# A new order for the lead-in of a gated linear attention with a folded maxout layer

## The chip, the cores and the metric

The kernel runs on one core of one Trainium2 chip. The metric is the device time of one execution in microseconds (us). Three runs of the kernel before gave 145.63, 147.28 and 148.08 us; their median is 147.28 us. One more execution was recorded by the hardware profiler; all durations below come from it.

## What is computed

For each of 4 batches and 8 heads (head size 48, 768 steps) a state of 48 x 48 is decayed by a gate and fed with an outer product, and then read:

```python
f = 1.0 / (1.0 + np.exp(-f_logit))
state = f[:, :, t, :, None] * state + np.einsum('bhd,bhe->bhde', k[:, :, t], v[:, :, t])
y[:, :, t] = np.einsum('bhd,bhde->bhe', q[:, :, t], state)
```

The 3072 x 384 result x then goes through a maxout layer of width 1024:

```python
h1 = x @ w1
h2 = x @ w2
g = np.maximum(h1, h2)
return (g @ w_out).astype(np.float32)
```

Inputs and output are float32.

## The kernel before, in words

**Tiles.** The 768 steps of a batch are cut into 6 chunks of 128. A tile i is chunk i // 4 of batch i % 4, so there are 24 tiles; tiles 0 to 3 have no earlier state. Within a tile the recurrence is written as products of matrices: the logarithms of the gates are summed along the chunk by a product with a triangular matrix (p_cum, L215), k and q are scaled by the exponentials of that sum (ei and ed; m_kp L248, m_qp L253), both are transposed by TensorE (p_tr, L258), their product a (p_a, L274) is masked (v_am, L284), and y (p_y, L313) is the masked product with v, with the old state added from the second chunk on. The state of the next chunk comes from sa (p_sa), tmp (v_tmp) and st (m_st, on GpSimd).

**The maxout layer.** max(h1, h2) is h2 + relu(h1 - h2). With wd = w1 - w2 (sub_wd, L178) a tile needs d = wd' x' in two halves of 512 rows (p_d, L343), a relu on ScalarE (a_g, L353), and then o = x · (w2 · w_out) + g · w_out (p_o, L359). The product w2 · w_out, called w2o, is made once at the start: w2 is cast to bf16 (cast_w2, L168), transposed in 8 blocks (tr_w2 L183, ev_w2T L188), w_out is cast in 4 parts (cast_wo, L174), and 12 pairs of products are summed (mm_w2o L191, ev_w2o L199).

**What sets the order.** The work of every engine is an order written out by hand as text. A word names an operation and a number its tile or part: "d0 -1" in the steady step is the first half of d for the tile before. PROLOGUE (L17) covers the start, STEP (L41) is repeated for i from FIRST_STEP on, and EPILOGUE (L48) ends it. The dictionary ops (in the function's last part) maps words to functions, and run (L435) leaves out what was already done. Each engine works through its own instructions in that order and waits at each for its inputs; nothing overtakes on VectorE, ScalarE or GpSimd. Transfers are issued from SP's queue: f, k, q and v of a tile (load, L147), a weight block of 128 rows (load_w, L156), half of w_out (load_wo, L159). A load is 192 KB in rows of 192 bytes, with nine buffers for each of the four inputs. In the steady step the store of tile i - 4 is issued from ScalarE ("outa"), all loads from SP: v two tiles ahead, q and k three, f four. The gate's last row of a tile from FL_ROW on is moved by a small transfer (a_fl, L232: "fl").

**The lead-in.** VectorE sets up masks and zeroed buffers; the f, q, k, v of tile 0 and the blocks of w2 are loaded first, then w_out in two halves, then w1. Nine products of zeros ("warm", L403) keep TensorE working. The suffixes name engines: w2ca is the cast on ScalarE, wdp the subtraction on GpSimd, kpv and qpv the scalings on VectorE (kp and qp without it: GpSimd).

PSUM has three pools: three buffers "s" for the attention, one "a", and three "mm" for the maxout layer and for w2's transposes.

Of the kernel before, what the change touches and what calls it, by code (L numbers as in the profile page):

```python
# [484 lines left out]
```

## Time and profile before

| What | Value |
|---|---|
| Median of three runs | 147.28 us (145.63 to 148.08) |
| Profiled execution | 145.47 us, of it the span 143.4 us |
| TensorE matmul busy | 129.9 us (91%) |
| VectorE busy | 107.0 us (75%) |
| ScalarE busy | 87.2 us (61%) |
| GpSimd busy | 69.0 us (48%) |
| Moved by transfers | 28.62 MB, mean 200 GB/s |
| A steady tile on TensorE | 4.90 us |

The span is the time between the first and the last instruction that the profile shows; the execution's own time is 2.07 us longer. A busy TensorE counts a product at half clock as busy, so its share is read together with the granted clock. In the listings, "L357" is the line of the kernel, "gT<-d" says which tile is written from which, "x48" how many instructions, and "idle before" with an arrow names what ended the wait. Transfers have no engine of their own in the listing; their issues stand under SPq and ACTq.

### The profile page before, as it was taken

The numbers are of one execution on the slowest core, as the hardware profiler recorded it, in microseconds if no ns is written. First come the engines' busy times: TensorE is split into PE (matmuls) and PEld (weight loads), VectorE is DVE, ScalarE is ACT, GpSimd is POOL, SyncE is SP. The second block draws the span as 40 slices with busy tenths as digits, with TensorE's granted clock in tenths as the row PEclk, the third lists the DMA queues.
The fourth block names the chain that finished last, engine by engine and source line by source line (L and its number), as shares of the span: only waits on it lengthen the run. The fifth ranks groups of instructions, "written<-read, shape, count | busy, mean of one in ns | idle before, by whom it ended". The sixth has DMA issues, their size and how long they took to land.

```text
span 143.4 us, 4345 instructions
## 1 busy us (share of the span) xinstructions
PE 129.9 (91%) x1756; PEld 100.3 (70%) x1756; DVE 107.0 (75%) x191; ACT 87.2 (61%) x183; POOL 69.0 (48%) x98
## 2 busy tenths in 40 slices
PE   0197499999999999999999999999999999999981
PEld 0044357688778877877887788778878887887771
DVE  7835985796889788877977897798779777976520
ACT  3572545967577566748666765767585757663440
POOL 8520060220748386566657655855685546442000
PEclk9999959999999999999999999999999999999999
DMA  4999999999999997998999999999999999971111
GB/s 94 274 347 389 342 307 169 188 198 166 188 175 179 194 209 202 218 196 190 221 191 207 197 204 218 224 172 235 228 210 189 218 214 220 171 215 59 55 55 55
DMA packets 105763, 28.62 MB, mean 200 GB/s; under 512 B 101520, under 2 KB 104720, under 8 KB 105744
## 3 DMA queue, kind: packets, MB, share of 16 engines
q1 hardware_dynamic: 103728, 25.60, 87.4%
q10 hardware_dynamic: 2016, 2.75, 5.7%
q8 instruction: 13, 0.21, 0.6%
q14 instruction: 6, 0.05, 0.1%
HBM read 23.59 MB, written 4.72 MB: 197 GB/s over the span
## 4 chain that ended last, share of the span: by engine, by line
PE 80%; DMA 10%; SPq 5%; ACT 3%; issue 1%; DVE 1%
PE o L368 27%; PE d L350 23%; PE tr L263 7%; DMA wo_f<-in_moe_w_out_dram 6%; PE a L281 5%; DMA ft<-in_f_logit_dram 4%; PE w2op L196 4%; PE y L326 3%; PE xtp L336 3%; PE cum L218 3%; PE y L321 2%; PE sa L295 2%; SPq L152 2%; SPq L161 1%; SPq L157 1%; ACT wo L176 1%
## 5 line engine op out<-in xcount | busy, mean ns | idle before, releaser
L350 PE MATMUL d<-xT,wd 128*128 128x128 bf16 x576 | 43.4, 220 | 0.5 <-DVE xT L340 0.4
L256 POOL TENSOR_TENSOR qp<-qt,ed 128x384 bf16<-128x384 f32 x22 | 22.1, 1002 | 45.0 <-ACT ed L230 30.3
L350 PEld LDWEIGHTS <-wd 128*128 128x128 bf16 x576 | 36.5, 114 | 4.5 <-issue 0.9
L368 PE MATMUL o<-wo,gT 128*128 128x384 bf16 x184 | 37.4, 325 | 0.0
L357 ACT ACTIVATE gT<-d 128x512 bf16<-128x512 f32 x48 | 28.9, 603 | 9.6 <-PE d L350 9.4
L286 DVE TENSOR_TENSOR am<-a,mask 128x1024 bf16<-128x1024 f32 x24 | 29.4, 1224 | 1.4 <-PE a L281 0.9
L340 DVE COPY xT<-xtp 128x384 bf16<-128x384 bf16 x24 | 8.6, 358 | 18.9 <-PE xtp L336 18.9
L368 PEld LDWEIGHTS <-gT 128*128 128x128 bf16 x184 | 16.2, 97 | 9.0
L310 POOL TENSOR_TENSOR st<-tmp,fl 64x192 bf16<-64x192 f32 x40 | 21.2, 530 | 2.7
L230 ACT ACTIVATE ed<-cum 128x384 f32<-128x384 f32 x24 | 11.8, 493 | 16.1 <-PE cum L218 15.0
L272 DVE COPY trs<-tr 128x1024 bf16<-128x1024 bf16 (+1 forms) x27 | 17.0, 631 | 4.1 <-PE tr L263 2.3
L331 ACT CAST x<-y 128x384 bf16<-128x384 f32 x24 | 11.5, 478 | 12.2 <-PE y L326 12.2
L237 POOL COPY flrow<-ed 32x384 f32<-32x384 f32 x16 | 17.8, 1113 | 1.0
L368 PE MATMUL o<-w2o,xT 128*128 128x384 bf16 x69 | 15.0, 326 | 0.0
L205 ACT ACTIVATE e<-ft 128x384 f32<-128x384 f32 x24 | 12.5, 525 | 3.6 <-DMA ft<-in_f_logit_dram 3.6
L251 DVE TENSOR_TENSOR kp<-kt,ei 128x384 bf16<-128x384 f32 x23 | 14.1, 614 | 0.7 <-ACT ei L226 0.5
L218 PE MATMUL cum<-ell,ut 128*128 128x384 bf16 x24 | 8.1, 339 | 7.0 <-ACT ell L209 7.0
L209 ACT ACTIVATE ell<-e 128x384 bf16<-128x384 f32 x24 | 12.5, 524 | 0.7
L373 DVE COPY ob<-o 128x384 f32<-128x384 f32 x23 | 12.6, 547 | 0.0
L226 ACT ACTIVATE ei<-cum 128x384 f32<-128x384 f32 x24 | 11.9, 496 | 0.0
L326 PE MATMUL y<-vb,am 128*128 128x48 bf16 x192 | 11.3, 184 | 0.2 <-DVE vb L213 0.2
L326 PEld LDWEIGHTS <-am 128*128 128x128 bf16 x192 | 9.7, 96 | 2.3 <-DVE am L286 0.4
(58 smaller groups left out, 173.1 us busy)
## 6 DMA issues: line engine op xcount, KB each, us to landing
ft<-in_f_logit_dram SPq DMA_DIRECT2D x24, 192.0 KB, 4.7
qt<-in_q_dram SPq DMA_DIRECT2D x24, 192.0 KB, 4.4
kt<-in_k_dram SPq DMA_DIRECT2D x24, 192.0 KB, 4.4
vt<-in_v_dram SPq DMA_DIRECT2D x24, 192.0 KB, 4.6
w_f<-in_moe_w_dram SPq DMA_DIRECT2D x6, 512.0 KB, 6.9
out_dram<-ob ACTq DMA_DIRECT2D x14, 192.0 KB, 3.4
out_dram<-ob SPq DMA_DIRECT2D x9, 192.0 KB, 2.6
wo_f<-in_moe_w_out_dram SPq DMA_DIRECT2D x2, 768.0 KB, 8.2
```

The costliest lines, as they stand in the source:

```text
L205: nc.scalar.activation(e, ld[i]["f"].rearrange("p h d -> p (h d)"), AF.Exp, scale=-1.0)
L237: nc.gpsimd.tensor_copy(row[:, :, 0:D, :].rearrange("s o d p -> s p o d"), st[i]["ed"][96:C, :].rearrange("s (p o d) -> s p o d", p=NP, o=2))
L251: eng.tensor_mul(s["kp"][:, :, 0:D], ld[i]["k"], s["ei"].rearrange("p (h d) -> p h d", h=H))
L256: eng.tensor_mul(s["qp"][:, :, 0:D], ld[i]["q"], s["ed"].rearrange("p (h d) -> p h d", h=H))
L272: nc.vector.tensor_copy(s["tr"][:, n:n + len(sel)], psum.pop(("tr" + sel, i)))
L286: nc.vector.tensor_mul(am.rearrange("p o n c -> p (o n) c"), psum.pop(("a", i)).rearrange("p o n c -> p (o n) c"), mask)
L310: nc.gpsimd.tensor_mul(st_b[b][(c + 1) % 2][r, :, e], st[i]["tmp"][r, :, e], st[i]["fl"][r, :].unsqueeze(2).to_broadcast([DP, NP, D]))
L326: nc.tensor.matmul(out=y[:, ds], lhsT=am[:, o, p, :], rhs=vb[:, ds], start=(c == 0), stop=(c == 0 or o == 1))
L350: nc.tensor.matmul(out=psum["d", half, i][:, n, :], lhsT=wd[:, j, ff(half * 4 + n)], rhs=st[i]["xT"][:, j, :], start=(j == 0), stop=(j == ...
L357: nc.scalar.activation(s["g"][:, half * 4:half * 4 + 4, :], psum.pop(("d", half, i)), AF.Relu)
L368: nc.tensor.matmul(out=psum["o", i], lhsT=l() if callable(l) else l, rhs=r, start=(n == 0), stop=(n == len(mms) - 1))
L373: nc.vector.tensor_copy(t, psum.pop(("o", i)))
```

## The change

The lead-in (the first four tiles and the weights) has another order, and the steady step starts at tile 4 instead of 7. w1 is loaded in halves of its columns and subtracted in halves (wdh on VectorE, wdhp on GpSimd). All w2 casts are on VectorE; the w_out casts are spread over VectorE (wocv), GpSimd (wocp) and ScalarE (woc); copies of w2's transposes and of w2o may be on ScalarE or VectorE (w2Tea, w2oev); v of tiles 1 to 3 is cast on ScalarE (va). Some transposes of w2 use the attention's PSUM buffers (w2Ts). q, k and v of some early tiles are issued from ScalarE's queue (lqa, lka, lva). There are 27 products of zeros, in four places, written to the "a" buffer (warma). In the steady step v is issued from ScalarE three tiles ahead, and the store of tile i - 4 from SP; q and k are issued two tiles ahead and f three. The small gate transfer is split from the copy that feeds it (fld, move_fl) and stands two steps later, and there are three flrow buffers. TensorE's order in the steady step and the epilogue is the same; loads and stores are moved there in the same way.

```diff
 PROLOGUE = """
-setup 0  setup 2  setup 1  lf 1  lf 0  lq 0  lw2 2  lk 0  lw2 0  lw2 1  lv 0  lwo 0  e 0
-lwo 1  e 1  ln 1  lk 1  ln 0  cum 0  cum 1  lw1 0  w2ca 2  warm 5  ei 0  lw1 2  fl 0  ed 0
-kp 0  ei 1  qpv 0  ed 1  fl 1  lw1 1  w2c 0  warm 3  warm 1  lq 1  w2ca 1  w2T 0  lf 2  w2T 7
-trk 0  w2Te 7  trq 0  w2T 4  trke 0  w2Te 0  trqe 0  w2T 5  w2T 1  a 0  lv 1  am 0  w2Te 1
-w2Te 4  v 0  lq 2  woc 2  w2T 2  y 0  w2Te 2  w2Te 5  woc 0  w2T 6  lk 2  w2T 3  woc 1  w2Te 6
-w2o 2  kpv 1  w2o 1  x 0  w2Te 3  trk 1  lf 3  wdp 0  woc 3  xT 0  trke 1  w2o 5  xTe 0
-w2o 4  w2o 7  w2o 10  lv 2  w2o 8  w2o 0  sa 0  wd 2  w2o 11  w2o 3  lk 3  w2oe 2  w2o 6
-w2oe 1  w2o 9  wd 1  w2oe 0  lq 3  qpv 1  d1 0  lf 4  e 2  trq 1  d0 0  ln 2  trqe 1  tmp 0
-lf 5  a 1  g0 0  v 1  cum 2  am 1  ed 2  lv 3  o0 0  g1 0  qp 2  ei 2  y 1  fl 2  lq 4  kpv 2
-o1 0  x 1  xT 1  trk 2  xTe 1  lk 4  e 3  trq 2  trke 2  d0 1  ln 3  trqe 2  ob 0  lk 5
-cum 3  a 2  v 2  ed 3  d1 1  g0 1  am 2  lv 4  ei 3  g1 1  o0 1  kpv 3  lq 5  y 2  qp 3
-o1 1  x 2  fl 3  xT 2  lv 5  e 4  tr 3  xTe 2  ln 4  sa 1  d0 2  tre 3  lf 6  ob 1  cum 4
-g0 2  a 3  d1 2  ed 4  lk 6  v 3  am 3  ei 4  g1 2  o0 2  lq 6  qp 4  e 5  tmp 1  y 3  fl 4
-o1 2  x 3  st 0  lf 7  kpv 4  ln 5  xT 3  tr 4  xTe 3  sa 2  lk 7  cum 5  tre 4  d0 3  ob 2
-a 4  lv 6  v 4  g0 3  d1 3  am 4  ei 5  ed 5  lv 7  g1 3  o0 3  qp 5  tmp 2  fl 5  y 4  kpv 5
-lq 7  o1 3  x 4  st 2  xT 4  lq 9  e 6  tr 5  xTe 4  st 1  sa 3  ln 6  d0 4  tre 5  lf 8
-ob 3  cum 6  g0 4  dq 4  a 5  v 5  d1 4  ed 6  am 5  lq 8  ei 6  qp 6  g1 4  o0 4  tmp 3  fl 6
-out 2  e 7  y 5  kpv 6  o1 4  x 5  lk 8  ln 7  xT 5  tr 6  xTe 5  sa 4  lf 9  d0 5  tre 6
-ob 4  cum 7  g0 5  dq 5  a 6  out 0  v 6  d1 5  ed 7  am 6  ei 7  lv 8  qp 7  g1 5  o0 5  tmp 4
-y 6  kpv 7  out 1  o1 5  x 6  st 3  fl 7  xT 6  tr 7  lk 9  e 8  xTe 6  sa 5  ln 8  tre 7
-lk 10  ob 5  v 7  lf 10
+setup 0  setup 2  setup 1  warma 9  lw2 0  lf 0  w2c 0  lw2 2  lw2 1  e 0  w2c 2  lf 1  w2c 1
+lva 0  w2T 1  w2Ts 7  v 0  ln 0  w2T 4  w2T 0  w2Te 1  lq 0  cum 0  w2Te 4  e 1  ei 0  w2Tea 0
+w2Ts 3  warma 3  ed 0  w2T 6  warma 4  qp 0  ln 1  lwo 0  w2Tea 7  lk 0  lw1h 2  w2Ts 5  warma 3
+lwo 1  w2Tea 5  fl 0  wocv 0  lqa 1  lka 1  kp 0  trq 0  w2T 2  warma 8  w2Te 3  trk 0  cum 1
+trke 0  wocp 1  w2Tea 6  trqe 0  lw1h 3  woc 2  lw1h 0  w2Te 2  w2o 1  fl 1  w2o 0  a 0  wocv 3
+ed 1  lw1h 4  w2o 7  am 0  qpv 1  lf 2  ei 1  lw1h 1  w2o 10  kpv 1  lw1h 5  lv 1  w2o 9  wdh 2
+w2o 5  lk 2  wdhp 4  y 0  lqa 2  x 0  w2o 11  w2o 3  trk 1  w2o 6  w2o 4  trq 1  wdh 0  trke 1
+xT 0  trqe 1  xTe 0  w2oev 1  w2o 2  w2o 8  lf 3  w2oev 2  a 1  e 2  w2oe 0  ln 2  sa 0  wdh 3
+d0 0  lv 2  wdh 5  am 1  g0 0  lqa 3  wdhp 1  tmp 0  cum 2  o0 0  d1 0  ed 2  ei 2  lk 3  fl 2
+va 1  kp 2  y 1  g1 0  lf 4  x 1  lv 3  o1 0  e 3  lq 4  xT 1  st 0  qpv 2  xTe 1  trk 2  ln 3
+trke 2  trq 2  d0 1  lk 4  trqe 2  lf 5  sa 1  a 2  cum 3  g0 1  ob 0  ed 3  lv 4  d1 1  am 2
+qpv 3  va 2  fl 3  o0 1  g1 1  y 2  o1 1  tmp 1  ei 3  x 2  kpv 3  xT 2  e 4  xTe 2  tr 3  d0 2
+ln 4  va 3  cum 4  tre 3  ed 4  dq 2  ob 1  lq 5  a 3  d1 2  am 3  g0 2  o0 2  y 3  g1 2  ei 4
+x 3  kpv 4  lk 5  lf 6  o1 2  xT 3  xTe 3  e 5  lva 5  qp 4  st 1  tr 4  tre 4  sa 2  fl 4  v 4
+lv 6  ob 2  ln 5  lva 6
 """
 
 STEP = """
-st -4  d0 -1  cum 1  dq -1  a 0  ed 1  d1 -1  g0 -1  am 0  lv 2  qp 1  fl 1  ei 1  lq 3  g1 -1  outa -4
-o0 -1  kpv 1  y 0  tmp -2  lk 3  o1 -1  x 0  e 2  xT 0  tr 1  ln 2  xTe 0  sa -1
-tre 1  ob -1  lf 4  v 1
+fld -1  st -4  d0 -1  cum 1  dq -1  a 0  ed 1  d1 -1  g0 -1  am 0  qp 1  fl 1  ei 1  lq 2  g1 -1  lva 3
+o0 -1  kpv 1  y 0  tmp -2  lk 2  o1 -1  x 0  e 2  xT 0  tr 1  ln 2  out -4  xTe 0  sa -1
+tre 1  ob -1  lf 3  v 1
 """
-FIRST_STEP = 7
+FIRST_STEP = 4
 FL_ROW = 4
 EPILOGUE = """
...
+st 15  d0 18  cum 20  dq 18  a 19  ed 20  d1 18  g0 18  am 19  qp 20  ei 20  lq 21  g1 18  lva 22  o0 18
+tmp 17  lk 21  st 16  out 15  y 19  kpv 20  o1 18  x 19  e 21  xT 19  tr 20  ln 21  xTe 19
+sa 18  d0 19  tre 20  fld 19  ob 18  lf 22  cum 21  dq 19  a 20  ed 21  v 20  d1 19  g0 19  am 20
+qp 21  ei 21  lq 22  g1 19  lva 23  o0 19  tmp 18  lk 22  st 17  fl 21  out 16  y 20  kpv 21  o1 19  x 20
+e 22  xT 20  tr 21  xTe 20  ln 22  sa 19  d0 20  tre 21  ob 19  lf 23  cum 22  
+dq 20  a 21  ed 22  v 21  d1 20  g0 20  am 21  ei 22  lq 23  out 17  g1 20  o0 20  tmp 19  lk 23  fl 22  y 21
...
-    flrow = [consts.tile([C, 2, DP, NP, 2], F32, name=f"flrow{n}") for n in range(2)]
+    flrow = [consts.tile([C, 2, DP, NP, 2], F32, name=f"flrow{n}") for n in range(3)]
...
-    def load(i, names="fkqv"):
+    def load(i, names="fkqv", eng=nc.sync):
...
-            nc.sync.dma_start(out=t, in_=SRC[name][b, :, sl, :].rearrange("h p d -> p h d"))
+            eng.dma_start(out=t, in_=SRC[name][b, :, sl, :].rearrange("h p d -> p h d"))
...
+    def load_w1h(n):
+        j, h = divmod(n, 2)
+        cs = slice(h * 4 * C, (h + 1) * 4 * C)
+        nc.sync.dma_start(out=w1_f[:, j, cs], in_=moe_w1[j * C:(j + 1) * C, cs])
...
-    def cast_wo(n):
+    def cast_wo(n, eng):
         s = slice(n * 2, n * 2 + 2)
-        nc.scalar.copy(wo[:, s, :], wo_f[:, s, :])
-
-    def sub_wd(j, eng=nc.vector):
-        eng.tensor_sub(wd[:, j, :], w1_f[:, j, :], w2_f[:, j, :])
+        if eng is nc.scalar:
+            nc.scalar.copy(wo[:, s, :], wo_f[:, s, :])
+        else:
+            eng.tensor_copy(wo[:, s, :], wo_f[:, s, :])
+
+    def sub_wd(n, eng=nc.vector):
+        j, h = divmod(n, 2)
+        cs = slice(h * 4 * C, (h + 1) * 4 * C)
+        eng.tensor_sub(wd[:, j, cs], w1_f[:, j, cs], w2_f[:, j, cs])
 
     psum = {}
 
-    def tr_w2(f):
-        ps = psum["w2T", f] = ps_m.tile([C, JG, C], BF16, name="w2tp", tag="mm")
+    def tr_w2(f, pool=ps_m, tag="mm"):
+        ps = psum["w2T", f] = pool.tile([C, JG, C], BF16, name="w2tp", tag=tag)
         for j in range(JG):
             nc.tensor.transpose(out=ps[:, j, :], in_=w2_h[:, j, ff(f)], identity=ident)
 
-    def ev_w2T(f):
-        nc.vector.tensor_copy(w2T[:, f, :], psum.pop(("w2T", f)).rearrange("p j c -> p (j c)"))
+    def ev_w2T(f, on_act=False):
+        ps = psum.pop(("w2T", f)).rearrange("p j c -> p (j c)")
+        if on_act:
+            nc.scalar.copy(w2T[:, f, :], ps)
+        else:
+            nc.vector.tensor_copy(w2T[:, f, :], ps)
+
+    folded = [0] * JG
 
     def mm_w2o(n):
         q, j = divmod(n, JG)
-        if q == 0:
+        if folded[j] == 0:
             psum["w2o", j] = ps_m.tile([C, dm], F32, name="w2op", tag="mm")
         for f in range(q * 2, q * 2 + 2):
+            folded[j] += 1
             nc.tensor.matmul(out=psum["w2o", j], lhsT=w2T[:, f, j * C:(j + 1) * C], rhs=wo[:, f, :],
-                             start=(f == 0), stop=(f == FG - 1))
-
-    def ev_w2o(j):
-        nc.scalar.copy(w2o[:, j, :], psum.pop(("w2o", j)))
+                             start=(folded[j] == 1), stop=(folded[j] == FG))
+
+    def ev_w2o(j, on_act=True):
+        if on_act:
+            nc.scalar.copy(w2o[:, j, :], psum.pop(("w2o", j)))
+        else:
+            nc.vector.tensor_copy(w2o[:, j, :], psum.pop(("w2o", j)))
...
-    def v_v(i):
+    def v_v(i, on_act=False):
         vb = st[i]["v"] = work.tile([C, dm], BF16, name="vb", tag="vb", bufs=5)
-        nc.vector.tensor_copy(vb, ld[i]["v"].rearrange("p h d -> p (h d)"))
+        src = ld[i]["v"].rearrange("p h d -> p (h d)")
+        if on_act:
+            nc.scalar.copy(vb, src)
+        else:
+            nc.vector.tensor_copy(vb, src)
...
-            row = flrow[i // 2 % 2][96:C, :, :, :, i % 2]
+            row = flrow[i // 2 % len(flrow)][96:C, :, :, :, i % 2]
             nc.gpsimd.tensor_copy(row[:, :, 0:D, :].rearrange("s o d p -> s p o d"),
                                   st[i]["ed"][96:C, :].rearrange("s (p o d) -> s p o d", p=NP, o=2))
-            if i % 2:
-                t = work.tile([C, NP, 2], F32, name="fl2", tag="fl2", bufs=4)
-                src = flrow[i // 2 % 2][C - 1:C].rearrange("s o d p t -> s (o d) (p t)")
-                nc.sync.dma_start(out=t.rearrange("s p t -> s (p t)"), in_=src)
-                st[i - 1]["fl"], st[i]["fl"] = t[:, :, 0], t[:, :, 1]
             return
         t = st[i]["fl"] = work.tile([C, NP], F32, name="fl", tag="fl", bufs=5)
         nc.scalar.activation(t, psum["cum", i][:, dm:dm + NP], AF.Exp, scale=-1.0)
+
+    def move_fl(i):
+        if FL_ROW <= i < T - B and i % 2:
+            t = work.tile([C, NP, 2], F32, name="fl2", tag="fl2", bufs=4)
+            src = flrow[i // 2 % len(flrow)][C - 1:C].rearrange("s o d p t -> s (o d) (p t)")
+            nc.sync.dma_start(out=t.rearrange("s p t -> s (p t)"), in_=src)
+            st[i - 1]["fl"], st[i]["fl"] = t[:, :, 0], t[:, :, 1]
...
-        if half == 0:
+        if "g" not in s:
...
-    def store(i, eng=nc.sync):
+    def store(i):
         c, b = divmod(i, B)
         r0 = b * S + c * C
-        eng.dma_start(out=out[r0:r0 + C, :], in_=st[i]["ob"])
+        nc.sync.dma_start(out=out[r0:r0 + C, :], in_=st[i]["ob"])
...
-    def warm(n):
-
-        ps = ps_m.tile([C, 512], F32, name="warm", tag="mm")
+    def warm(n, pool=ps_m, tag="mm", shape=(C, 512)):
+        ps = pool.tile(list(shape), F32, name="warm", tag=tag)
         for _ in range(n):
-            nc.tensor.matmul(out=ps, lhsT=ell_b[1][:, 0:2, :].rearrange("p h d -> p (h d)"),
+            nc.tensor.matmul(out=ps.rearrange("p o n c -> p (o n c)")[:, 0:512] if len(shape) > 2 else ps,
+                             lhsT=ell_b[1][:, 0:2, :].rearrange("p h d -> p (h d)"),
                              rhs=ell_b[1].rearrange("p h d -> p (h d)"), start=True, stop=True)
...
+        "lva": lambda i: load(i, "v", nc.scalar), "lqa": lambda i: load(i, "q", nc.scalar),
+        "wocv": lambda n: cast_wo(n, nc.vector), "wocp": lambda n: cast_wo(n, nc.gpsimd),
+        "w2T": tr_w2, "w2Ts": lambda f: tr_w2(f, ps_s, "s"),
...
```

## Prediction

> **What bounds the kernel now.** I read the page first, then busy time by stretch, then the order of instructions in the first 30 us, then the issues and landings of each tile's loads.
>
> The chain that ended last, and the stretches (columns: PE, weight load, DVE, ACT, POOL busy with counts, granted clock, DMA share, GB/s):
>
> ```profile
> PE 80%; DMA 10%; SPq 5%; ACT 3%; issue 1%; DVE 1%
> ```
> ```profile
> 8.00:20.00 12.00, 9.11 (x72) 5.12 (x71) 7.72 (x18) 6.91 (x13) 2.73 (x2) 0.93 1.06 369
> 20.00:45.00 25.00, 24.96 (x327) 18.77 (x326) 19.89 (x33) 16.13 (x37) 9.08 (x12) 0.97 1.13 181
> 45.00:80.00 35.00, 34.82 (x505) 27.92 (x506) 28.63 (x51) 23.14 (x51) 21.80 (x29) 1.00 1.01 203
> 80.00:120.00 40.00, 40.00 (x579) 31.99 (x577) 32.30 (x58) 27.02 (x59) 25.08 (x32) 1.00 1.03 209
> ```
> From 20 to 129 us TensorE has no gap that counts (0.22 us in all), and a tile takes 4.90 us: the d products start at 73.44, 78.34 and 83.24. So a new order can only win in the lead-in, or lose later. Beside that, the transfer engines are full: 181 GB/s while only tile loads move, 369 while weights are among them. Two resources run neck and neck.
>
> The lead-in, in order of time (start, duration, then what):
>
> ```profile
> 14.56 1.23 DVE L286 TENSOR_TENSOR am<-a,mask 128x1024 bf16<-128x1024 f32 x1 [0.49 <-PE a L281]
> 16.01 2.30 ACT L176 CAST wo<-wo_f 128x768 bf16<-128x768 f32 x3 [3.79 <-DMA wo_f<-in_moe_w_out_dram]
> 18.27 2.35 POOL L179 TENSOR_TENSOR wd<-w_f 128x1024 bf16<-128x1024 f32 x1 [7.96 <-DMA w_f<-in_moe_w_dram]
> 19.04 3.45 PE L196 MATMUL w2op<-wo,w2T 128*128 128x384 bf16 x12
> 27.23 0.37 PE L326 MATMUL y<-vb,am 128*128 128x48 bf16 x8
> ```
> ```profile
> 19.00:20.00 1.00, 1.00 (x7) 0.49 (x5) 1.00 (x3) 0.42 (x1) 1.00 (x1) 0.50 1.06 351
> 20.00:21.00 1.00, 1.00 (x5) 0.50 (x4) 1.00 (x1) 0.00 (x0) 0.62 (x1) 0.50 1.34 225
> ```
> w_out lands at 16.0, the w2·w_out products run from 17.6, the first d at 23.95, and y of tile 1 at 27.23. I use that last instant as the milestone: by then d1 0, d0 0, a 1, cum 2 and the first six o products of tile 0 are done, in both orders. Part of w2o runs at half clock, about 18.5 to 21.6: some 1.55 us lost.
>
> **What the Trainium skill says.** "TensorE: Matmul & The Clock Gate", Part 1 (The HAM clock gate): TensorE gets half its clock after an idle window of about 3.4 us and the full clock after about as long busy. The trace agrees: 0.50 after the thin stretch 14 to 17.6 us. "DMA: Bandwidth & Descriptors", Issuing engines are not separate DMA queues: moving an issue to ScalarE saves issue time only, not bandwidth. Same page, Queues, rings and completion order: each transfer engine goes round-robin over the queues it has work for. No run here has loads on two queues, so neither is shown. Same page, Specifications: rows under 512 B don't reach line rate; 181 against 369 GB/s agrees.
>
> **Cost of transfers.** Up to 20 us, 6 x 254 + 12 x 369 KB = 5.95 MB moved, of which 4.72 MB weights, so 1.23 MB or 6.3 tile loads of 197 KB. A load at 181 GB/s is 1.09 us; 6.3 take 6.8 of the 18 us from 2.0 on, leaving 11.2 for the weights: 1.25 us for 512 KB, 1.87 for 768, 0.62 for 256. Landing comes some 1.2 us after. Test on before: five loads 5.45, w2 3.74, w_out 3.74, from 2.0: 14.9, plus 1.2 is 16.1, and the trace has 16.0.
>
> **The change, part by part.**
>
> *Weights and first tiles.* New SP order ahead of the end of w_out: w2 3.74, w_out 3.74, half of one w1 block 0.62, loads f0, f1, q0, v0, k0 5.45: lands at 16.75. But q 1 and k 1 now go out on ScalarE's queue, after the ln, casts and fl before them in its order, at about 13.8 by adding up those durations; by round-robin they take half of the engines while the second w_out half moves: 0 to 2.2 us more. I take 1.05: **w_out at 17.8** instead of 16.0 (16.75 to 18.9). The column halves of w1 that d0 0 needs follow: 17.8 - 1.2 + the rest of q1/k1 1.1 + two halves 1.25 + 1.2 = 20.2 landed, then 1.2 on POOL (half of 2.35) is 21.4: hidden, since d0 comes later. The cover is the DVE queue below; without it that costs nothing before 21.4.
>
> *Zero products.* 27 in place of 9, in the PE queue, 0.22 us each at full clock (0.43 cold, by the first nine). They stand where PE waits for weights until 17.8, so they cost nothing there, and w2o runs at full clock: the 1.55 us above comes back. If PE were not waiting, 18 more would cost 3.9 us; the wait for w_out hides them.
>
> *Casts over several engines.* Now DVE's order puts a cast of w_out (wocv 3) ahead of am 0, so VectorE waits for w_out with all of tile 0 and 1 behind it. From that landing to y of tile 1 its queue is: wocv 0.51 (0.75 of 0.68), am 1.23, q and k products of tile 1 2 x 0.55, two wd halves 2 x 0.83 (half of 1.67), two copies of tr 2 x 0.42, xT 0.36, two w2o copies 2 x 0.55 (as ob), two wd halves 1.66, am 1.23: **9.7 us**. In the same time PE needs less: 20 w2o products x 0.16 + y, tr, xT, a, sa 1.3 = 4.6 to d0 0, and then d0 0.67, cum 0.27, o 0.98, d1 0.67: 7.2. So VectorE, not PE, sets the milestone: 17.8 + 9.7 = 27.5, against 27.23. In before am 0 was done at 15.8, and DVE sat partly idle. **+0.3 us**; PE's regained clock is swallowed by this queue. Bounds: w_out at 16.75 gives 26.4 (-0.8), at 18.9 with 0.5 for DVE beside POOL gives 29.1 (+1.9).
>
> *Steady steps.* The PE order is word for word the same: 4.90 us. ScalarE's queue now issues v (three tiles ahead) instead of the store. The store took 338 ns there; a load takes at least 427 on SP and 877 at the median, where the full queue holds it. ScalarE then has 0.56 us idle before x. Up to 0.34 + 0.56 = 0.9 us the issue is hidden: I take 0.45, cost 0; the upper end is in rival two. The store moves to SP, where nothing computes behind it; only q, k and f loads queue.
>
> *Loads' lead.* Load f of tiles 6 to 9 landed 0.4, 1.0, 1.1, 1.5 us ahead of its exp, f 10 at 63.0 just as wanted (0.8 us wait), later tiles 0.9 to 3.9 ahead; 0.6 more lies between ln and cum. Counting issues: ahead of f 7 stood 27 loads, now 28 or 29 and a store (+1.6 to +2.7 us); ahead of f 10, 40 and four stores, the same now; ahead of f 23, 91 and 16, now 93 and 17 (+2.6). So the lead is used up but hardly exceeded: **+0.1**. A lead-in gain of more than about 1 us could not be kept here.
>
> *Fl transfer split off, third flrow buffer.* SP waits less; the row is needed two steps on, landing takes 3.4 us: 0. Epilogue: same PE order, 0.
>
> Sum against the profiled execution: 145.47 (span 143.4 and 2.07 around it) + 0.3 + 0.1 = 145.9. That execution is 1.81 below the median of the runs, 147.28; so I forecast **147.6**.
>
> **Rivals.** *One, faster: the lead-in is really shorter.* If q 1 and k 1 don't delay w_out (16.75) and DVE runs without contention, 26.4 or -0.8; if loads on two queues also fill the dips where SP is held 2 us and more (76 GB/s from 35 to 36 us), the tile loads keep up, another 1 us off the DVE queue by waits I overrate: -2. Gives 145.3. For it: the half clock and those dips. Against: the same bytes on the same engines, VectorE's queue.
> *Two, slower: ScalarE is held by its own load issues.* SP's were held over 1.7 us eleven times in 96. If ScalarE's queue behaves like that, each v issue over 0.9 us delays x, xT and d: 17 issues in the steady steps; at a mean of 1.1 us it costs 17 x 0.2 = 3.4, and two of 2.4 us cost 3. With prologue losses of 0.6, +4: 151.3. Decisive from a mean of about 1.1 us. Against: the store issued at 85.23 on ScalarE took 0.38 while SP's load of 85.21 was held 1.79, so the queues don't hold each other.
> *Three, it changes nothing* is close to my forecast: the new order is just as much tied to w_out's landing.
>
> **Chances.** Runs of this kernel differ by 1.7%, so 2% (2.9 us) is about what a measurement tells from no change. Forecast and its neighbours 0.60 (145.0 to 149.5), faster rival 0.17 (142.5 to 146), of which 0.12 pass 2%; slower rival and a worse lead-in 0.23 (149.5 to 154). Same takes 0.62, slower 0.26. The range leaves a tenth at each end: 144.6 to 151.5.
>
> **What would show it.** Last w_out half landing near 17.8; the DVE group wocv, am 0 back to back after it; clock 1.00 from 17 to 22 us; y of tile 1 near 27.5; d period 4.90; ScalarE's v issues near 0.45 us. I am wrong if w_out lands by 16.5 and y of tile 1 starts before 26 (faster), or if x waits after ScalarE's issues, or exp for f by more than 1 us per tile (slower).

## The result, and the profile after

The changed kernel takes 151.05 us at the median (150.27 to 152.97, four runs); the kernel before, beside it on the same chip, 147.68 us (145.63 to 149.19). The ratio is 1.029, with a 95% interval of 1.021 to 1.037: slower, where I had forecast 147.6 us and no difference. The profiled execution took 150.98 us, its span 149.2 us; the span before was 143.4 us, so 5.8 us have to be found. (The profiles of e7, e15 and e18 below are of executions 2 to 3% longer than the fastest of the same kernel, so they show that a wait is there, but no difference in time is explained by them.)

The chain that ended last and the same stretches as before (PE, weight load, DVE, ACT, POOL busy with counts, granted clock, DMA share, GB/s), of the changed kernel:

```profile
PE 79%; DMA 10%; SPq 6%; DVE 1%; ACT 1%; issue 1%; DVEq 0%
```
```profile
8.00:20.00 12.00, 9.71 (x63) 5.54 (x63) 3.66 (x10) 4.86 (x13) 2.78 (x4) 0.72 1.12 314
20.00:45.00 25.00, 22.03 (x264) 15.43 (x264) 18.94 (x32) 13.61 (x32) 8.07 (x9) 0.93 1.20 198
45.00:80.00 35.00, 35.00 (x511) 28.07 (x510) 28.26 (x51) 22.95 (x49) 21.09 (x26) 1.00 1.01 204
80.00:120.00 40.00, 40.00 (x586) 32.04 (x586) 32.24 (x59) 27.00 (x58) 25.36 (x33) 1.00 0.98 195
```

From 45 us on TensorE has no gap, and a tile takes 4.90 us as before. Everything is lost ahead of that. From 20 to 45 us TensorE is busy for 22.0 us instead of 25.0; VectorE does half as much from 8 to 20 us (3.7 us instead of 7.7); and the granted clock is 0.72 and 0.93 where it was 0.93 and 0.97. My milestone, y of tile 1, starts at 32.68 instead of 27.23 (5.45 us later), and the copy xT of tile 1, used below since it is easy to follow from tile to tile, at 34.5 instead of 28.6.

The lead-in of the changed kernel in order of time:

```profile
15.46 0.52 ACT L223 ACTIVATE ell<-e 128x384 bf16<-128x384 f32 x1 [2.45 <-issue]
15.74 0.38 ACTq L146 DMA_DIRECT2D qt<-in_q_dram  x1
17.09 1.89 PE L426 MATMUL warm<-ell 128*128 128x512 bf16 x8
17.75 0.38 ACTq L146 DMA_DIRECT2D kt<-in_k_dram  x1
19.24 0.75 DVE L292 COPY trs<-tr 128x512 bf16<-128x512 bf16 x2 [4.20 <-PE tr L283]
19.98 1.27 POOL L183 TENSOR_TENSOR wd<-w_f 128x512 bf16<-128x512 f32 x1 [3.27 <-DMA w_f<-in_moe_w_dram]
20.17 1.49 DVE L178 CAST wo<-wo_f 128x768 bf16<-128x768 f32 x1
23.44 0.56 DVE L276 TENSOR_TENSOR qp<-qt,ed 128x384 bf16<-128x384 f32 x1 [0.64 <-DMA qt<-in_q_dram]
25.11 0.56 DVE L271 TENSOR_TENSOR kp<-kt,ei 128x384 bf16<-128x384 f32 x1 [1.11 <-DMA kt<-in_k_dram]
25.73 0.49 PE L283 MATMUL tr<-ident,kp 128*128 128x128 bf16 x4 [1.85 <-DVE kp L271]
26.02 1.49 PE L207 MATMUL w2op<-wo,w2T 128*128 128x384 bf16 x4
32.68 0.36 PE L346 MATMUL y<-vb,am 128*128 128x48 bf16 x8
```

The reader is to see four things: ln 1 (ell) sits behind a wait of 2.45 us; VectorE waits 4.20 us for the transposes of tile 0, which stand behind the eight zero products; its next cast takes 1.49 us while GpSimd's wd runs beside it; and q 1 and k 1, issued at 15.74 and 17.75, are there only at 23.3 and 25.0. TensorE waits 1.85 us for the product with k 1; its clock, 1.00 from 16 to 25 us, then drops, and four w2o products take 1.49 us instead of 0.81; the stretches of 1 us that answer to 19 and 20 us before lie at 26 to 29 us now:

```profile
26.00:27.00 1.00, 1.00 (x7) 0.50 (x5) 1.00 (x3) 0.10 (x1) 0.00 (x0) 0.50 1.36 186
28.00:29.00 1.00, 1.00 (x6) 0.50 (x4) 1.00 (x3) 0.00 (x0) 0.00 (x0) 0.50 0.91 179
```

### The profile page after: what moved, and what is told of

It reads as the page before. It is cut to its first block, busy times and chain, and to the rows that moved or that the text cites. A ratio compares the mean times of both kernels' runs of the same rounds, so it can differ in the third digit from the quotient of the medians.

```text
span 149.2 us, 4383 instructions
## 1 busy us (share of the span) xinstructions
PE 136.5 (91%) x1774; PEld 102.6 (69%) x1774; DVE 107.0 (72%) x192; ACT 85.4 (57%) x183; POOL 70.8 (47%) x101
## 4 chain that ended last, share of the span: by engine, by line
PE 79%; DMA 10%; SPq 6%; DVE 1%; ACT 1%; issue 1%; DVEq 0%
PE o L388 28%; PE d L370 24%; PE tr L283 7%; PE a L301 5%; DMA kt<-in_k_dram 5%; DMA wo_f<-in_moe_w_out_dram 5%; SPq L160 3%; PE y L346 3%; PE xtp L356 3%; PE cum L236 2%; PE y L341 2%; PE sa L315 2%; PE w2op L207 2%; SPq L146 2%; PE o L409 1%; SPq L151 1%
## 5 line engine op out<-in xcount | busy, mean ns | idle before, releaser
L276 POOL TENSOR_TENSOR qp<-qt,ed 128x384 bf16<-128x384 f32 x21 | 21.1, 1004 | 46.8 <-issue 39.4
L330 POOL TENSOR_TENSOR st<-tmp,fl 64x192 bf16<-64x192 f32 x40 | 21.7, 542 | 2.6
L292 DVE COPY trs<-tr 128x1024 bf16<-128x1024 bf16 (+1 forms) x27 | 16.9, 630 | 6.8 <-PE tr L283 5.0
L219 ACT ACTIVATE e<-ft 128x384 f32<-128x384 f32 x24 | 12.7, 527 | 7.6 <-DMA ft<-in_f_logit_dram 7.6
L223 ACT ACTIVATE ell<-e 128x384 bf16<-128x384 f32 x24 | 12.6, 524 | 3.1 <-issue 2.5
L271 DVE TENSOR_TENSOR kp<-kt,ei 128x384 bf16<-128x384 f32 x22 | 12.3, 559 | 1.6 <-DMA kt<-in_k_dram 1.1
L393 DVE COPY ob<-o 128x384 f32<-128x384 f32 x23 | 12.6, 547 | 0.0
L426 PE MATMUL warm<-ell 128*128 128x512 bf16 x27 | 10.1, 529 | 1.8 <-DVE ell L118 1.5
L346 PE MATMUL y<-vb,am 128*128 128x48 bf16 x192 | 11.2, 183 | 0.0
L283 PE MATMUL tr<-ident,kp 128*128 128x128 bf16 x96 | 9.4, 221 | 1.8 <-DVE kp L271 1.8
```

Of the source, the lines that this page charges most:

```text
L219: nc.scalar.activation(e, ld[i]["f"].rearrange("p h d -> p (h d)"), AF.Exp, scale=-1.0)
L223: nc.scalar.activation(ell[:, :, 0:D], st[i]["e"].rearrange("p (h d) -> p h d", h=H), AF.Ln, bias=1.0)
L276: eng.tensor_mul(s["qp"][:, :, 0:D], ld[i]["q"], s["ed"].rearrange("p (h d) -> p h d", h=H))
L283: nc.tensor.transpose(out=ps[:, n, p, :], in_=src[:, 2 * p:2 * p + 2, :].rearrange("p h d -> p (h d)"), identity=ident)
L292: nc.vector.tensor_copy(s["tr"][:, n:n + len(sel)], psum.pop(("tr" + sel, i)))
L330: nc.gpsimd.tensor_mul(st_b[b][(c + 1) % 2][r, :, e], st[i]["tmp"][r, :, e], st[i]["fl"][r, :].unsqueeze(2).to_broadcast([DP, NP, D]))
```

## The experiments

The ratios are to the kernel before on the same chip.

### Parts of the lead-in, in the changed kernel

**e1: a tile of zeros of its own.** The zero products read ell_b[1], which ln 1 writes; so ln 1 waits for them.

```diff
-lhsT=ell_b[1][:, 0:2, :].rearrange("p h d -> p (h d)"),
+lhsT=zero[:, 0:128],
```

> The kernel after, with a tile of zeros of its own for the zero products, so that ln of tile 1 no longer waits until they have read ell. Theory A (late q 1 and k 1 behind ScalarE's waiting ln, and VectorE waiting behind TensorE's queue, make the loss): ln 1 moves from 15.46 to about 13 us, the issue of k 1 from 17.75 to about 15.5, its landing from 25.1 to about 23; y of tile 1 from 32.7 to about 30.7; time 151.0 to about 149.2. Theory B (the zero products on TensorE themselves make the loss): less than 0.5 us. Theory C (loads and stores moved in the steady step make the loss): no change.

151.12 us, 1.037 (1.030 to 1.044). ln 1 no longer waits (13.03), and k 1 is issued at 16.00 instead of 17.75; but q 1 and k 1 arrive at 23.7 and 25.3, y of tile 1 is at 32.87, and theory A's 149.2 us is missed. Issuing them earlier didn't bring them earlier. The loads from SP were no faster there: v 1 and k 2, issued at 18.41 and 19.09 in the changed kernel, landed 7.3 and 8.4 us later. In both kernels k 1 is issued within 0.06 us of the landing of the transfer eight before it (17.73, the second half of w_out; 15.94 in e1): no more than eight transfers are under way, for a reason seen at e13. With eight under way and a landing every 0.97 us (16 between 15 and 31 us), a load takes some 7.8 us by my estimate, whichever queue issues it.

**e2: without the eight zero products ahead of the transposes of k 0.**

```diff
-w2T 2  warma 8  w2Te 3  trk 0
+w2T 2  w2Te 3  trk 0
```

> The kernel after without the last group of 8 zero products (ahead of the k transposes of tile 0). Theory A: the transposes and VectorE's w_out cast come some 1.9 us earlier, but q 1 and k 1 still land at 23.4 and 25.1 and hold the q and k products of tile 1, so the time falls by at most 0.7 us. Theory B: y of tile 1 and the time 1.9 us or more earlier (149). Theory C: no change.

151.63 us, 1.042 (1.036 to 1.049). am 0 is at 18.22 instead of 21.59, and y of tile 0 3 us earlier. All of it is lost again in the wait for q 1 and k 1:

```profile
22.34 1.18 DVE L276 TENSOR_TENSOR qp<-qt,ed 128x384 bf16<-128x384 f32 x1 [2.90 <-DMA qt<-in_q_dram]
24.52 0.56 DVE L271 TENSOR_TENSOR kp<-kt,ei 128x384 bf16<-128x384 f32 x1 [1.00 <-DMA kt<-in_k_dram]
```

y of tile 1 is at 32.98. So, as theory A has it, the late q 1 and k 1 are enough for the whole delay.

**e3: q 1 and k 1 from SP, behind k 0.**

```diff
-lk 0  lw1h 2 ...  lqa 1  lka 1
+lk 0  lq 1  lk 1  lw1h 2 ...
```

> The kernel after with q and k of tile 1 issued from SP right behind k 0, ahead of the second half of w_out, in place of ScalarE's queue. Theory A: both land by about 17 us, w_out's second half about 1.5 us later than 17.75; VectorE no longer waits 0.64 and 1.11 us for them; y of tile 1 near 31, the time 1.5 us less (149.5). Theory B and theory C: no change, or 1 us slower by the later w_out.

151.1 us, 1.036 (1.029 to 1.044). They arrive at 16.2 and 16.9, the second half of w_out at 21.0 instead of 17.75, and y of tile 1 is at 31.27: 1.4 us won. Two things stand out. VectorE's two wd halves took 3.44 us beside GpSimd's two (see e10). And the 1.7 us that xT of tile 1 had won were gone by tile 10.

**e9: the loads of the lead-in from SP, in the order of the kernel before.**

```diff
-warma 9  lw2 0  lf 0 ... (loads spread through the lead-in, three from ScalarE)
+warma 9  lf 1  lf 0  lq 0  lw2 2  lk 0  lw2 0  lw2 1  lv 0  lwo 0  lwo 1  lk 1  lw1h 0  lw1h 1
+lw1h 4  lw1h 5  lw1h 2  lw1h 3  lq 1  lf 2
```

> The changed kernel with the loads of the lead-in all on SP and in the order of the kernel before (f 1, f 0, q 0, w2 2, k 0, w2 0, w2 1, v 0, w_out, k 1, the six w1 halves, q 1); engines, zero products and steady steps stay as changed. Theory A, the order of the loads is most of the loss: the second half of w_out lands at 16.0 to 16.5 instead of 17.75 and k 1 before 18, q 1 at about 21.5; y of tile 1 at 29 to 30 instead of 32.68, the time 148.5. Theory B, the order of the engines (casts and copies of w_out, w2 and wd among VectorE, ScalarE and GpSimd) is the loss: y of tile 1 stays above 31.5, the time above 150.

148.88 us, 1.026 (1.022 to 1.030); y of tile 1 at 30.08, xT at 31.8. The order of the loads is about half of the lead-in's loss (2.6 of 5.45 us): near theory A's milestone, but not most of the loss. Here, too, 0.7 us are lost again at tile 10.

**e10: e3, and all of wd on VectorE.**

```diff
-w2o 5  lk 2  wdhp 4  y 0 ... wdh 5  am 1  g0 0  lqa 3  wdhp 1
+w2o 5  lk 2  wdh 4  y 0 ... wdh 5  am 1  g0 0  lqa 3  wdh 1
```

> e3 (q 1 and k 1 on SP) and beside it the two halves of wd that GpSimd forms in the lead-in formed on VectorE. Theory A, VectorE is held while GpSimd subtracts: the wd halves take 0.64 us each, the cast of w_out 0.56, so VectorE does six halves in 3.9 us where e3 needed 3.44 for two of them; copy xT of tile 1 at 31.5 to 32.2 instead of 32.8. Theory B, the two don't hold each other: the halves on VectorE stay at 1.2 to 1.7 us and the copy of tile 1 comes at 34 or later. The whole time stays at 150.5 to 151.5 in A, since e3 kept none of its lead after tile 10; in B 152.

150.2 us, 1.034 (1.030 to 1.039). First e3, then e10, VectorE's wd halves:

```profile
23.58 3.44 DVE L183 TENSOR_TENSOR wd<-w_f 128x512 bf16<-128x512 f32 x2
```
```profile
22.91 1.89 DVE L183 TENSOR_TENSOR wd<-w_f 128x512 bf16<-128x512 f32 x3
26.57 1.29 DVE L183 TENSOR_TENSOR wd<-w_f 128x512 bf16<-128x512 f32 x2
```

A half takes 0.63 us alone and 1.72 beside GpSimd: theory A. y of tile 1 comes at 30.34, 0.9 us ahead of e3, though the last half now stands behind am 1 and d1 0 waits 1.44 us for it. xT of tile 1 is at 32.2; then the tile steps of 6.84 and 5.56 us at tiles 8 and 10 give 2.6 us back.

**e14: all mended at once** (e9, own zeros, without the eight, all of wd on VectorE, am 0 ahead of wocv 3).

```diff
-trk 0 ... a 0  wocv 3  ed 1  w2o 7  am 0
+trk 0 ... a 0  ed 1  w2o 7  am 0  wocv 3
```

> The changed kernel with its lead-in mended in five places: loads in the order of the kernel before and from SP (as e9), all of wd on VectorE, a tile of zeros of its own for the zero products, the eight of them ahead of the transposes of k 0 left out, am 0 ahead of the last cast of w_out. Theory A, these are the causes: ln 1 by 13.5, am 0 by 19 and y of tile 1 at 26.0 to 28.0 (e9 30.1, changed 32.7), so no later than the 27.2 of the kernel before; the copy xT of tile 1 at 27.5 to 29.5. Theory B, the engines' new order costs something else: y of tile 1 at 29 or later. The time: if the new step keeps a lead, 145.5 to 147; if it gives it back as e3 and e10 did, 148.5 to 150.

151.22 us, 1.038 (1.031 to 1.044). am 0 comes at 19.43, but VectorE then waits 1.53 us for q 1, has no gap from 22.65 to 31.5, and y of tile 1 is at 31.32, later than in e9: d1 0 waits 1.73 us for the last wd half behind am 1. Theory A fails here: the causes found don't add up, because with each repair VectorE's queue, or what waits behind it, is next.

### The same parts, put into the kernel before

**e7: seven zero products** in the wait for w_out, from a tile of their own.

```diff
-w2T 5  w2T 1  a 0  lv 1
+w2T 5  w2T 1  a 0  warms 7  lv 1
```

> The kernel before with 7 more products of zeros (from a tile of zeros of their own) in TensorE's wait behind a of tile 0. Theory A: the clock stays at 1.00 from 17 to 22 us, the w2 times w_out products take 1.5 us less, y of tile 1 is limited by w1's landing and VectorE, 0.5 to 1.5 us earlier; the time falls by no more than 1 us, since f loads allow about 1 us. If the half clock costs nothing, no change at all.

146.78 us, 1.004 (1.001 to 1.007). The clock is 1.00 from 18 to 22 us, and twelve w2o products take 2.11 us instead of 3.45:

```profile
19.25 2.11 PE L198 MATMUL w2op<-wo,w2T 128*128 128x384 bf16 x12
26.70 0.37 PE L328 MATMUL y<-vb,am 128*128 128x48 bf16 x8
```

y of tile 1 comes 0.5 us earlier. Later in this execution exp is late for f three times between 44 and 64 us (2.5 us in all, where the kernel before has one wait of 0.8), and x five times after 98 us; that these waits took the gain is likely, not shown. Zero products do what I said, in the right place, and still win nothing in time.

**e8: k 1 from ScalarE's queue.**

```diff
-lwo 1  e 1  ln 1  lk 1  ln 0
+lwo 1  e 1  lka 1  ln 1  ln 0
```

> The kernel before with k of tile 1 issued from ScalarE (behind exp of tile 1, at about 6 us) in place of SP at 8.24 us. If a load of short rows on ScalarE's queue gets half of the engines beside SP's weights, it lands by about 10 us instead of 16.9. If the engines alternate packet by packet between the queues, 192 bytes against 4 KB or more, it lands later than 14 us although it was issued 2 us sooner, and the weights are hardly delayed. Time within 1 us of before in both cases.

148.8 us, 1.019 (1.013 to 1.025), so not within 1 us. Issued at 4.88, k 1 landed at 12.9, 8.0 us later, between both expectations; from SP's queue it had landed at 16.9, 8.7 us after its issue. Half of the engines' time would have been less: at 181 GB/s a load takes 1.09 us, at half of that 2.2, and with the prediction's 1.2 us to landing 3.4. What share it got, the packets tell. From 9 to 10.5 us SP's queue (q1) moved weights and ScalarE's (q10) k 1 (packets, MB, share of the engines' time):

```profile
q1 hardware_dynamic: 146, 0.54, 92.2%
q10 hardware_dynamic: 120, 0.02, 7.7%
```

The packets are nearly as many, but k 1's are rows of 192 bytes and the weights' mostly rows of 4 KB. The milestone suffered: w2's last block landed 1.7 us later (12.9 instead of 11.2), VectorE's k product of tile 1 then ran beside GpSimd's wd (1.47 us instead of 0.55), and y of tile 1 came 3.0 us late, at 30.27.

### The steady step

**e4: the kernel before with the new loads and stores**, without the split gate row.

```diff
-am 0  lv 2  qp 1  fl 1  ei 1  lq 3  g1 -1  outa -4 ... lk 3 ... lf 4
+am 0  qp 1  fl 1  ei 1  lq 2  g1 -1  lva 3 ... lk 2 ... out -4 ... lf 3
```

> The kernel before with the loads and stores of the new steady step and epilogue alone: v from ScalarE three tiles ahead, stores from SP, q and k two ahead, f three; the lead-in as before and the small gate transfer where it was. Theory A: within 1 us of before, a tile still 4.90 us. Theory C: 3 us slower, with exp waiting for f or x waiting behind ScalarE's issues.

159.32 us, 1.092 (1.083 to 1.100). Neither theory had the reason: SP waits for GpSimd's row with all later loads behind it, 22.1 us between 40 and 130 us:

```profile
SPq L242 <- POOL flrow L237: 22.1, 6, 4.4
```

So the split isn't a trifle: the new load order needs it.

**e5 and e12: the whole new step behind the old lead-in**, the second a repeat. Both have the row of tiles 4 and 5 at the end of the lead-in.

```diff
-lk 10  ob 5  v 7  lf 10
+lk 10  ob 5  v 7  lf 10  lv 9  fld 5
+fld -1  st -4 ... (STEP of the changed kernel)
```

> The kernel before with the whole new steady step and epilogue: as the kernel with the moved loads and stores alone, and also the split of the small gate transfer (two steps later) and the third flrow buffer. Theory A (the whole loss of the change is in the lead-in): within 1 us of before; the 13 us of the run without the split came from SP waiting for the gate's row with the next loads behind it. Theory C (ScalarE's v loads and SP's stores themselves starve the tile loads): 5 us or more slower than before, with exp waiting for f.

> The kernel of e5 (the kernel before with the new steady step) profiled a second time. If the 4.0 us that its lead-in lost in e5 are chance, the copy xT of tile 1 starts nearer 28.6 than 32.6 and the time is 147 to 149; if they belong to that kernel, it starts above 31.5 again and the time is 151 to 152.

e5: 151.8 us, 1.038 (1.030 to 1.046), so theory A fails; e12, one execution: 150.46 us. In e5 the lead-in took 3.9 us longer than before (xT of tile 1 at 32.6), in e12 it didn't (28.5); but there 5.1 us went at tile 8, and both end alike (last xT at 141.1 and 141.7; 136.4 before). First e5, then e12, in the lead-in:

```profile
13.15 0.63 PE L265 MATMUL tr<-ident,kp 128*128 128x128 bf16 x4
18.93 2.49 DVE L253 TENSOR_TENSOR kp<-kt,ei 128x384 bf16<-128x384 f32 x1
22.20 4.05 PE L196 MATMUL w2op<-wo,w2T 128*128 128x384 bf16 x12
```
```profile
12.93 0.39 PE L265 MATMUL tr<-ident,kp 128*128 128x128 bf16 x4
18.06 0.55 DVE L253 TENSOR_TENSOR kp<-kt,ei 128x384 bf16<-128x384 f32 x1
20.00 2.35 PE L196 MATMUL w2op<-wo,w2T 128*128 128x384 bf16 x12
```

In e5 the transposes of tile 0 already take the length of half clock (its recorded clock says 1.00 all the same), so VectorE comes to the k product of tile 1 0.9 us later; it then falls beside GpSimd's wd (18.66 to 21.01), takes 2.49 us, and the w2o products behind it take that length too. The wait at tile 8 is for the row, which I had sent a whole step later than the changed kernel does. e13 mends that.

**e11: the kernel before once more.**

> The kernel before, unchanged, profiled a second time. If the length of its lead-in is its own, the copy xT of tile 1 starts within 0.5 us of the 28.6 of the first profile. If the lead-in depends on where TensorE's half clock falls, it starts up to 3 us elsewhere, and the transposes of w2 take 0.63 instead of 0.39 us.

145.34 us in one execution; xT of tile 1 at 28.8, last at 136.6. Its lead-in doesn't wander; that of e5 did.

**e13: the same with the row in its old place.**

```diff
-qp 5  tmp 2  fl 5  y 4
+qp 5  tmp 2  fl 5  fld 5  y 4
```

> The kernel before with the whole new steady step (v from ScalarE's queue, q, k and f one tile later, store on SP, gate row split off, third flrow buffer), and the gate row of tiles 4 and 5 sent where the kernel before sends it. Theory A, the step costs nothing by itself and the stall of e12 came from that late row: the last copy xT at 136.4 to 137.5, no wait over 1.5 us at tiles 7 to 12, the ratio 0.995 to 1.010. Theory B, the step has less lead and stalls when the lead-in doesn't delay TensorE: waits for f or for a gate row of 3 us or more at tiles 8 to 14, the ratio 1.025 to 1.04.

150.8 us, 1.037 (1.030 to 1.044): theory B by its time and its tiles, but not by what is waited for. With xT of tile 1 at 29.1 the step loses 3.44, 1.53 and 0.86 us at tiles 9, 10 and 12. What TensorE waits for is x on ScalarE:

```profile
70.51 0.45 ACTq L152 DMA_DIRECT2D vt<-in_v_dram  x1
71.00 0.48 ACT L333 CAST x<-y 128x384 bf16<-128x384 f32 x1 [4.07 <-DMA kt<-in_k_dram]
71.54 0.34 PE L338 MATMUL xtp<-ident,x 128*128 128x128 bf16 x3 [3.27 <-ACT x L333]
...
87.65 0.40 ACTq L152 DMA_DIRECT2D vt<-in_v_dram  x1
88.09 0.48 ACT L333 CAST x<-y 128x384 bf16<-128x384 f32 x1 [1.49 <-DMA ft<-in_f_logit_dram]
```

The 1.53 us of tile 10 follow from the first stall: TensorE's clock is down (0.69 and 0.50, the first figure after the busy times):

```profile
72.00:74.00 2.00, 2.00 (x29) 1.64 (x28) 1.70 (x4) 0.63 (x2) 0.00 (x0) 0.69 1.10 225
74.00:76.00 2.00, 2.00 (x20) 1.58 (x19) 1.47 (x2) 1.49 (x4) 1.48 (x2) 0.50 1.10 250
```

x doesn't read k or f. The load of v just ahead of it in ScalarE's order waits, and x behind it. In the built program an issue names, beside its data, one or two of eight transfer semaphores (counters that tell of a landing):

```
SP       q  waits DMAHW1     ScalarE  v  waits DMAHW5, DMAHW1
SP       out waits DMAHW2    ScalarE  x  waits PE
SP       f  waits DMAHW3
SP       q  waits DMAHW4
```

They go round by the number; so an issue waits for the transfer eight back in the program's order to land. The trace agrees: v at 70.51 follows by 0.08 us the landing of the k that had its semaphore last, and of 132 such issues in the changed kernel none starts before that landing. On SP only later transfers stand behind such a wait; on ScalarE it holds x. The same pair, an issue on ScalarE and then x late "for" a load that it doesn't read, stands at the lost steps of e3 (2.57 us), e5 (1.29), e9 (1.32) and e10 (2.55 and 1.28), and after a store issued from ScalarE in e6, e7, e15 and e16. Neither the kernel before nor the changed one has it anywhere from 35 us on; in its lead-in the changed kernel has it once, where k 1's issue holds ScalarE for 1.36 us until 18.16.

**e16, e17, e18: which part of the step.** e16 is the kernel before with the split row and third buffer alone; e17 is e13 with v two tiles ahead instead of three; e18 is e13 with q and k three and f four tiles ahead, as before.

```diff
+fld -1  st -4  d0 -1 ...                       (e16, loads and store as before)
-... lq 2  g1 -1  lva 3   ->   ... lq 2  g1 -1  lva 2   (e17)
-... lq 2 ... lk 2 ... lf 3   ->   ... lq 3 ... lk 3 ... lf 4   (e18)
```

> The kernel before with the load of the gate row split off from the copy and sent at the head of the next step, and a third flrow buffer; loads and stores as before. If the split costs nothing: the last copy xT at 136 to 137.5, the ratio 0.993 to 1.010. If a row sent later is too late when the lead is 5 to 7 us: waits of GpSimd's state update for the row of 2 us or more and a ratio above 1.02.

> e13 with v loaded from ScalarE's queue two tiles ahead, not three. If v asked for too early is what pushes q and f back, q 10 is issued before 61 (e13 63.5) and the stall at tiles 9 to 12 falls from 5.8 us to under 2, the ratio to 1.00 to 1.015. If q, k and f a tile later are the cause, the stall stays at 4 us or more and the ratio at 1.025 to 1.04.

> e13 with q and k loaded three and f four tiles ahead as in the kernel before; v stays on ScalarE's queue three ahead, stores on SP, the row split. If q, k and f a tile later are the cause, no stall above 1.5 us is left and the ratio is 1.00 to 1.015. If v asked for too early is the cause, f or q is still late by 3 us or more in all and the ratio is 1.02 to 1.04.

| Kernel | Ratio | x late behind an issue (us, times) | Mean lead of a load, tiles 13 to 20 (us) | f 20 issued | Last xT |
|---|---|---|---|---|---|
| before | 1 | 0 | 6.9 | 103.6 | 136.4 |
| e16 | 1.008 (1.003 to 1.012) | 1.37, 1 | 6.7 | 104.3 | 137.3 |
| changed | 1.029 (1.021 to 1.037) | 0 | 12.5 | 106.2 | 142.1 |
| e17 | 1.027 (1.019 to 1.036) | 5.42, 4 | 9.4 | 104.0 | 140.1 |
| e13 | 1.037 (1.030 to 1.044) | 5.56, 2 | 12.6 | 107.4 | 142.7 |
| e18 | 1.052 (1.040 to 1.063) | 10.15, 5 | 15.0 | 104.1 | 145.3 |

A lead is the time from the issue of a load to the start of the instruction that uses it, averaged over f, q, k and v. The loads are issued at the same pace in all six, f of tile 20 within 3.8 us; what differs is how far the work runs behind them. The split row is nearly free. In e17 the stall at tiles 9 to 12 fell to 1.5 us, as expected if v is the cause, but tiles 13 to 15 lost 1.9 more, and q 10 was issued at 62.6 and not before 61: v a tile earlier may be part of it (the intervals of e17 and e13 overlap), but not all. e18 is no faster than e13, so q, k and f asked for later are not the cause; how its stalls compare with e13's is not shown. What is common to e13, e17 and e18 and absent in e16 is v issued from ScalarE and the store from SP. Which of the two matters more was not tried.

The lead also tells when a gain in the lead-in is lost. In the changed kernel, e14, e9, e3, e10 and e13, which all have the new step, the mean lead at tiles 5 to 7 is 12.3, 12.5, 10.3, 9.8, 9.1 and 7.4 us, and tiles 5 to 20 lose 0.0, 0.0, 0.7, 2.1, 2.6 and 5.8 us; at tiles 13 to 20 all six have a lead of 12.4 to 12.7. The less lead the new step starts with, the more it loses until it has that lead.

**e6 and e15: the old step behind the changed lead-in**, as in e3 and as in e14; the row stays split.

```diff
-fld -1  st -4 ... am 0  qp 1 ... lq 2  g1 -1  lva 3 ... lk 2 ... out -4 ... lf 3
+fld -1  st -4 ... am 0  lv 2  qp 1 ... lq 3  g1 -1  outa -4 ... lk 3 ... lf 4
```

> The kernel after with q and k of tile 1 from SP, and with the steady loads and stores of before (v two ahead from SP, q and k three, f four, stores from ScalarE). Theory A: the 1.7 us gained at tile 1 by q and k from SP, and lost again at tile 10, are kept, 149.4. If what was lost at tile 10 is a lack of transfer capacity and not of order, the same wait comes back at some tile between 6 and 12, and the time stays at 151.

> e14 with the loads and stores of the old steady step (the row transfer stays split). Theory A, loads are short in either order when TensorE starts early: f waits of 2 to 6 us in all between tiles 6 and 18, the time within 1 us of e14. Theory B, the old order has more lead: no wait over 1 us, the time 145 to 146.5.

152.29 us, 1.045 (1.040 to 1.050), and 152.51 us, 1.039 (1.033 to 1.045). e6 starts the tiles 2.3 us ahead of the changed kernel (xT of tile 1 at 32.2) and loses 2.1 us at tile 13 and 0.5 to 0.6 at each of tiles 17 to 19; e15 (34.5) loses 1.2, 0.3 and 0.5 us at tiles 17 to 19. In both x is late behind the store issued from ScalarE. So neither half of the old kernel rescues the other. No version measured beats the kernel before; e7 and e16 come within 1% of it.

## Why the prediction was wrong

- **What bounds the kernel: right.** Two resources run neck and neck, and a gain in the lead-in could not be kept: e3, e9 and e10 gave back 2.1, 0.7 and 2.6 us by tile 10. I looked for the loss in exp waiting for f; it came in x instead.
- **w_out at 17.8: right** (17.75: issued at 10.55, 7.2 us to landing), and so was its cost in the sum.
- **q 1 and k 1 "take half of the engines": wrong.** I let them go out at 13.8; they went out at 15.74 and 17.75 and landed 7.6 and 7.3 us later. That time alone doesn't tell their share, since loads from SP took as long (e1); the packets of e8 do, 7.7% beside weights. The Trainium skill, "DMA: Bandwidth & Descriptors", Queues, rings and completion order, says that the engine changes queues by the packet; I read that as half of the time. The trace of e8 fits the page, with 120 packets against 146, and not my reading of it. I asked what these loads do to w_out, not when they land themselves.
- **The zero products cost nothing: wrong in two ways.** They read a buffer that ln 1 writes (2.45 us of wait, though q 1 goes out only 0.15 us earlier without it, e1), and the eight at 17.09, the last of five groups (9, 3, 4, 3 and 8, not four as said above), push back the transposes of k 0, so that VectorE's cast starts at 20.17 and not at 17.8. The clock was up from 17 to 22 us as forecast, but didn't stay up: it is 0.50 again after TensorE's wait for k 1, and eight of the 24 w2o products take 2.93 us instead of 1.62. That is as much as the 1.34 us that the half clock cost before by e7's measure (3.45 instead of 2.11; I had put 1.55).
- **VectorE's queue sets the milestone: the mechanism was right, the size wrong.** This is the step that failed. I gave it 9.7 us from the landing of w_out; it took 14.9. Behind the difference stand 2.42 us until the cast starts, 0.64 and 1.11 for q 1 and k 1, 0.76 for a transpose and 0.40 for w2o at half clock (together 5.33), and 0.98 more for the cast beside GpSimd; four wd halves at 0.64 instead of 0.83 gave 0.76 back. (That is 0.35 more than the difference; neighbouring instructions overlap at their ends, as the cast until 21.66 and am 0 from 21.59.) I had summed durations and put the waits at nothing. That two wd halves and GpSimd exclude each other stands in the skill, "SBUF — State Buffer", Who interferes with whom: a VectorE instruction with both inputs in SBUF and a GpSimd instruction that reads SBUF don't run side by side. e3 and e10 agree for the subtraction; I had put 0.5 us for it at the end of my range, e3's two halves alone lost 2.2. Of casts the page says it for a faster mode of copying; the cast here took 1.49 us against 0.56 alone.
- **Steady steps 4.90 us, ScalarE's v issue hidden: right for this kernel** (issues at 0.38 us). But rival two's mechanism is there, in another form than I priced: not the issue's own time, but the wait ahead of it. It decides nothing here, as far as the runs show, because the late lead-in has given every load a long lead: 12.3 us at tiles 5 to 7, against 7.4 in e13. Take the delay away and it costs 5.8 us (e13), the fallen clock included. My argument against it, a store's issue of 0.38 us, looked at the issue and not at the wait. That rival two's 151.3 us lies beside the measured 151.05 is luck: its waits are not in this kernel, and its 0.6 us for the lead-in were 5.4. The skill ("DMA: Bandwidth & Descriptors", Issuing engines are not separate DMA queues) says that issuing elsewhere saves only the sequencer's time; the trace agrees for the 0.38 us of an issue, and shows the price, x behind a wait of 4.07 us.
- **Loads' lead +0.1 and the split row 0:** near enough for the first; the row costs about 1.1 us alone (e16), and without the split the new loads cost 9% (e4).
- **The sum:** 145.47 + 0.3 + 0.1 (with the 1.81 us it makes 147.7, not 147.6) was to be 150.98. The 5.1 us missed are the milestone's: 32.68 instead of 27.5. None of the signs that I named for "slower" appeared; the milestone itself was the sign.

What stays open: what remains between 27.2 and 30.1 us for y of tile 1 when the loads come in the old order (e9) was not split further, and why e5's transposes were slow at 13 us, when e12's were not, is not known.

## What to carry to other kernels

Sum the queue of the engine that sets a milestone with its waits, not its durations: for each input, when does it land, what stands ahead of its producer, and how many transfers are already under way? Ask of a load or store that is moved to a computing engine what it may wait for before it is issued, and what stands behind it there. And where engine and transfers are both at their limit, a delay in one hides a fault of the other: judge each half of a change on the kernel before, too, since the halves' losses don't add.

## What was not expected of the hardware

- With up to eight transfers under way, a load of 192 KB took 7.3 to 9.3 us to land from ScalarE's queue (q 1 and k 1 in the changed kernel, e1, e2 and e8) and 7.3 to 9.2 from SP's (v 1 and k 2 in the first three), and its landing hardly followed its issue (k 1 issued at 16.00, 16.91 and 17.75 landed at 25.3, 24.4 and 25.0).
- Rows of 192 bytes on one queue beside rows of 4 KB on another got 7.7% of the engines' time (e8, 9 to 10.5 us).
- A wd half on VectorE took 0.63 us alone and 1.72 beside GpSimd's; a cast of 128 x 768 0.56 and 1.49; a k product of 128 x 384 0.55 and 2.49 (e12, e5).
- The issue of a load took 0.38 us on ScalarE, but with it held for an earlier transfer from SP, the engine stood idle for up to 4.07 us (e13).
- In two executions of one kernel (e5, e12) the lead-in differed by 4 us and the end by 0.6.
